# Attention and two expert layers in one kernel: one branch behind the first expert's blocks, another order of the ending, later zeros and weights, and tokens routed in groups of 8, 8, 4, 2 and 2 tiles

## The chip, the cores and the metric

The kernel runs on one core of one Trainium2 chip. The metric is the time of an execution on the device, in microseconds; of several runs the median counts.

## The reference: what is computed

Three layers follow one another. N is 3072 tokens of width 384, there are 8 experts of hidden width 1024, and a dense layer of hidden width 2048.

```python
# 1: gated linear attention, 4 batches x 8 heads, 768 steps, 48 wide
for t in range(S):
    state = alpha[:, :, t, :, None] * state + k[t] (x) v[t]
    y[:, :, t] = q[t] @ state
# 2: each token goes to one expert, the arg max of a cosine
logits = xn @ en.T / tau
expert_idx = argmax(logits); gate_w = softmax(logits)[expert_idx]
out[mask] = gate_w[mask, None] * (relu(x[mask] @ w1[e]) @ w2[e])
# 3: dense layer with an ELU
h = x @ w_in
g = np.where(h > 0.0, h, np.exp(np.minimum(h, 0.0)) - 1.0)
return g @ w_out
```

## The kernel before, in words

**Attention** (`fast`, lines 608 to 707) works on 24 tiles of 128 tokens (6 chunks of time by 4 batches). One pass of its loop serves several tiles at different stages: `load` and `load_v` fetch tile i+3; `stR` and `stA` make running products of alpha for tile i+2 (two scans on VectorE, lines 311 and 321) and multiply k and q with them on GpSimd (`Kh` line 314, `Qh` line 323); `stS` forms scores of tile i+1 (TensorE, line 351) and `stP` masks them (VectorE, line 358); `stC` forms the output of tile i and the update of the state; `stD` turns the output of tile i-1 into rows of the token table and logits (line 419). The loop has 22 passes (i = 0 to 21); `ending` (lines 736 to 793) finishes the last two tiles in an order of its own.

**Routing.** Tiles are routed in groups (`GROUPS`, line 35): five of four and two of two. `stR1` finds each token's expert and its norm, `stR2` its place among the rows of that expert (small matmuls, line 500, and three VectorE instructions), `stX` and `gates` the gate. A group's instructions go into a list `todo`, and each pass takes up to 12 of them. In the loop `stR1` of a group starts two passes after its last tile, `stR2` three passes after it and ahead of `stS` and `stT`, `stX` four passes after it. `scale_x` multiplies a tile's rows with the gate (ScalarE, line 518) and `put` scatters them by an indirect DMA of GpSimd into the table `xs` (line 528), at most one tile a pass.

**Other loads.** At pass 1 SP asks for the first six pieces of expert weights (`load_w`, line 156), at passes 2 to 5 it writes zeros into two experts' parts of `xs` a pass (`fill`, line 543). At passes 4 to 15 a piece of weights is split into a high and a low part (`split_piece`, ScalarE line 172, VectorE line 175), after which the next piece is asked for. Each engine works its own queue in the order of the program; SP's queue issues nearly all loads.

**Into the experts.** Rows of tiles 0 to 21 are read back from `xs` for expert 0 (`load_rows`, line 246); those of the last two tiles come in by a one-hot matmul (`first_x`, line 540), added up in the same PSUM tiles `t0`. Then come two branches that all engines take: line 798 leads to `general` and the filling of rare short experts, line 1111 to `overflow` for an expert with more than 432 tokens. Each begins with a register load on each engine (lines 797 and 1110) from a flag that `pack` computes (lines 820 to 846). Behind them `moe1` (lines 848 to 959) transposes the rows of expert 0 (`turn`, lines 877, 880, 881), and runs 64 blocks (expert e, hidden slice f): `mm1` is the first layer (lines 892 to 898), `mm2` the second (lines 907 to 909), one block later. At f = 6 SP loads a register and copies the expert's token numbers to `idl` (lines 939 and 940). Dense weights come as 64-bit words (`load_d`, line 196) and are decoded on the way. `moe2` is the dense layer; its output goes out by indirect DMAs.

Of the kernel before, what the change touches and what calls it, by code (L numbers as in the profile page):

```python
# [8 lines left out]
F32 = mybir.dt.float32  # L9
# [9 lines left out]
N, DM = B * S, H * D  # L19
# [15 lines left out]
GROUPS = [list(range(i, i + 4)) for i in range(0, 20, 4)] + [[20, 21], [22, 23]]  # L35
# [24 lines left out]
def fused_kernel(ctx, tc, qk, a, v, emb, w12, wi, wo, cst, sel, cols, out):  # L60
# [34 lines left out]
    bad_i = const.tile([1, 1], I32, name="bad_i")  # L95

# [161 lines left out]
    def attention():  # L258
        with ExitStack() as st:
# [14 lines left out]
            rhsX = gp.tile([128, NP, CW + E], F32, name="rhsX")  # L274
            ss = gp.tile([128, NT], F32, name="ss")
            chk = gp.tile([C2, NT, NP, 2], F32, name="chk")
            ones = gp.tile([128, 1], F32, name="ones")
            tick = gp.tile([1, 1], F32, name="tick")
# [162 lines left out]
            todo, putq, urgent, late = [], [], [], []  # L441

# [48 lines left out]
            def stR2(g):  # L491
# [3 lines left out]
                r = ps1.tile([128, 4, E], F32, tag="psT" if g == NG - 2 else "psR", name="psR")[:, :n]  # L495
# [50 lines left out]
            def general():  # L546
# [13 lines left out]
                rv = wk.tile([128, TB, DE], F32, tag="yT", name="row_v")  # L560
# [47 lines left out]
            def fast():  # L608
# [42 lines left out]
                gated = set()  # L651
                last = {tiles[-1]: g for g, tiles in enumerate(GROUPS)}
                tail = NT - 2
                for i in range(tail):
                    load(i + 3)
                    load_v(i + 3)
                    if i == 1:
                        load_w(2 * PIECES)
                    if 2 <= i < 2 + E // 2:
                        for e in (2 * i - 4, 2 * i - 3):  # L660
                            fill(e, zero, FULL if e else 0)
                    if i - 3 in last:
                        todo[:0] = stR2(last[i - 3])
                    stS(i + 1)
                    stT(i + 1)
# [6 lines left out]
                    stP(i + 1, 1)  # L672
                    while late:
                        late.pop(0)()
# [61 lines left out]
            def ending():  # L736
# [4 lines left out]
                r = stR2(g2 - 1)  # L741
                run(urgent, r)
# [54 lines left out]
            odd = nc.values_load(odd_i[0:1, 0:1], min_val=0, max_val=4 * E + C2)  # L797
            with tc.If(odd > 0):
                bad = nc.values_load(bad_i[0:1, 0:1], min_val=0, max_val=C2)
                with tc.If(bad > 0):  # L800
                    with tc.manual_schedule():
                        general()
                        run(pack(sm, ps1))
                zero = wk.tile([128, CAPR], F32, tag="P", name="zero")
                nc.vector.memset(zero, 0.0)
                for e in range(E):
                    n_low = nc.values_load(low_i[0:1, e:e + 1], min_val=0, max_val=FULL // 64)
                    with tc.If(n_low > 0):
                        n_e = nc.values_load(cnt_i[0:1, e:e + 1], min_val=0, max_val=N)
                        with tc.For_i(0, n_low, 1) as s:  # L810
                            row = nc.s_assert_within(n_e + s * 64 + e * REG, 0, E * REG - 64)
# [380 lines left out]
```

## Time and profile before

| | us |
|---|---|
| median of 3 runs | 866.92 |
| lowest and highest | 863.48, 867.87 |
| the profiled execution | 860.85 |
| its span, first to last instruction | 858.9 |

The profile is of one execution. It gives for each engine the time in which it was busy, in all and by stretches, and what ended each wait. PE is TensorE, with PEld its weight loads; DVE is VectorE, ACT ScalarE, POOL GpSimd and SP SyncE; a q behind a name is that engine's queue of register loads, branches and DMA issues. PEclk is the granted clock of TensorE as a share of 2.4 GHz. The stages can be told by their lines: attention up to about 164 us, the ending and the routing of the last tiles up to about 185, the experts from 194 to about 450, and the dense layer after that.

### The profile page before, as it was taken

What the parts mean: (1) busy time and instruction counts of PE and PEld (TensorE: products, weight loads), DVE (VectorE), ACT (ScalarE), POOL (GpSimd) and SP (SyncE); (2) the same over time, 40 slices, a digit from 0 to 9 for tenths busy, and PEclk for the clock granted to TensorE, in tenths of its full rate; (3) what the DMA queues carried; (4) which work ended last, traced back from release to release, by engine and by line L of the source; (5) the groups of instructions that cost most, each with busy time, mean ns of one, the idle gap of its engine ahead of it and who ended that gap; (6) DMA issues with size and microseconds to landing.
All of it is one profiled execution on the core that took longest, in us unless ns stands there. A gap on an engine that the chain in (4) does not pass through costs nothing.

```text
span 858.9 us, 13084 instructions
## 1 busy us (share of the span) xinstructions
PE 803.1 (94%) x4880; PEld 726.0 (85%) x4880; DVE 548.8 (64%) x1054; ACT 361.3 (42%) x763; POOL 200.1 (23%) x218
## 2 busy tenths in 40 slices
PE   7697888859998998999999999999999999999996
PEld 5697877728988988999998889999999999999995
DVE  7699999833676776777636766545545555455442
ACT  2365756522544544545535544333323333333231
POOL 6334656631233333333200002002002001000102
PEclk7798989798999999999999999999999999999999
DMA  9978678231676776778400000000000000000000
GB/s 243 309 223 237 204 214 243 75 111 48 149 195 169 153 202 168 138 240 191 88 1 1 0 1 37 1 1 38 0 1 28 10 1 15 23 0 2 36 1 37
DMA packets 45249, 82.33 MB, mean 96 GB/s; under 512 B 11624, under 2 KB 18024, under 8 KB 45168
## 3 DMA queue, kind: packets, MB, share of 16 engines
q1 hardware_dynamic: 42096, 71.88, 32.1%
q0 software_dynamic: 3072, 9.45, 2.9%
q8 instruction: 41, 0.67, 0.4%
q14 instruction: 40, 0.33, 0.1%
HBM read 69.10 MB, written 12.22 MB: 95 GB/s over the span
## 4 chain that ended last, share of the span: by engine, by line
PE 63%; DMA 5%; DVE 4%; ACT 3%; issue 1%; SPq 0%; POOLq 0%; POOL 0%; DVEq 0%; ACTq 0%
PE h L1044 20%; PE o L1067 7%; PE o L1065 7%; PE o L1066 7%; PE y L907 4%; PE y L908 3%; DMA raw<-in_wi_dram 3%; PE h L892 3%; PE h L894 3%; PE y L909 3%; PE h L893 3%; DMA raw<-in_wo_dram 1%; PE t L875 1%; DVE dlo L231 1%; DVE g L1050 1%
## 5 line engine op out<-in xcount | busy, mean ns | idle before, releaser
L1046 DVE TENSOR_SCALAR mn<-h 128x512 f32<-128x512 f32 x96 | 66.3, 690 | 139.6 <-PE h L1044 139.6
L1047 ACT ACTIVATE mn<-mn 128x512 f32<-128x512 f32 x96 | 60.7, 633 | 171.3 <-DVE mn L1046 171.3
L1067 PE MATMUL o<-dwo,gl 128*128 128x384 f32 x384 | 129.5, 337 | 1.5 <-DVE gl L1054 1.4
L1066 PE MATMUL o<-dlo,gh 128*128 128x384 f32 x384 | 128.3, 334 | 0.0
L1065 PE MATMUL o<-dwo,gh 128*128 128x384 f32 x384 | 128.3, 334 | 0.0
L1076 POOL DMA_INDIRECT out_dram<-ob,ids x24 | 23.5, 981 | 390.7 <-DVE ob L1071 231.6
L1044 PE MATMUL h<-xh,dwi 128*128 128x512 f32 x288 | 112.9, 392 | 0.6 <-ACT x2T L921 0.6
L1044 PE MATMUL h<-xh,dlo 128*128 128x512 f32 x288 | 113.1, 393 | 0.0
L1044 PE MATMUL h<-xl,dwi 128*128 128x512 f32 x288 | 112.5, 392 | 0.0
L1053 ACT ACTIVATE gh<-g 128x512 fp32r<-128x512 f32 x96 | 60.7, 633 | 78.5 <-DVE g L1050 78.5
L897 ACT ACTIVATE hh<-h 128x432 fp32r<-128x432 f32 x64 | 33.9, 530 | 104.7 <-PE h L894 102.6
L1050 DVE SCALAR_TENSOR_TENSOR g<-mn,h 128x512 f32<-128x512 f32 x96 | 66.1, 689 | 15.4 <-ACT mn L1047 15.3
L1065 PEld LDWEIGHTS o<-dwo,gh 128*128 128x128 f32 x384 | 72.0, 187 | 4.2
L1066 PEld LDWEIGHTS o<-dlo,gh 128*128 128x128 f32 x384 | 72.0, 187 | 4.0
L898 DVE SCALAR_TENSOR_TENSOR hl<-h,hh 128x432 fp32r<-128x432 f32 x64 | 38.7, 605 | 55.8 <-ACT hh L897 55.8
L907 PE MATMUL y<-hh,whi 128*128 128x432 f32 x192 | 71.3, 371 | 3.3 <-ACT hh L897 3.3
L175 DVE TENSOR_TENSOR wlo<-raw,whi 128x512 fp32r<-128x512 f32 x96 | 71.4, 768 | 4.5 <-ACT whi L172 4.5
L215 POOL TENSOR_SCALAR dg<-dg 128x384 f32<-128x384 f32 x32 | 40.9, 1279 | 142.9 <-ACT dg L214 142.6
L1067 PEld LDWEIGHTS o<-dwo,gl 128*128 128x128 f32 x384 | 72.2, 188 | 2.4 <-DVE gl L1054 2.1
L908 PE MATMUL y<-hl,whi 128*128 128x432 f32 x192 | 69.2, 360 | 2.9 <-DVE hl L898 2.9
L892 PE MATMUL h<-xh,whi 128*128 128x432 f32 x192 | 69.1, 360 | 0.0
L894 PE MATMUL h<-xh,wlo 128*128 128x432 f32 x192 | 69.1, 360 | 0.0
(204 smaller groups left out, 1581.5 us busy)
## 6 DMA issues: line engine op xcount, KB each, us to landing
raw<-in_w_dram SPq DMA_DIRECT2D x96, 256.0 KB, 3.6
qk<-in_qk_dram SPq DMA_DIRECT2D x24, 448.0 KB, 6.8
vt<-in_v_dram SPq DMA_DIRECT2D x24, 352.0 KB, 6.8
raw<-in_wi_dram SPq DMA_DIRECT2D x16, 384.0 KB, 4.4
raw<-in_wo_dram SPq DMA_DIRECT2D x16, 384.0 KB, 4.4
at<-in_alpha_dram SPq DMA_DIRECT2D x24, 226.2 KB, 4.7
xr<-xs SPq DMA_DIRECT2D x7, 576.0 KB, 11.8
xs<-zero SPq DMA_DIRECT2D x7, 288.8 KB, 7.5
```

The costliest lines, as they stand in the source:

```text
L175: nc.vector.tensor_tensor(l[:, sl], r, h[:, sl].bitcast(F32), op=ALU.subtract)
L892: nc.tensor.matmul(ps, wh, xh[:, kk], start=(kk == 0), stop=False)
L894: nc.tensor.matmul(ps, wl, xh[:, kk], start=False, stop=(kk == KD - 1))
L907: nc.tensor.matmul(acc[e][d], wh, hh, start=(f == 0), stop=False)
L908: nc.tensor.matmul(acc[e][d], wh, hl, start=False, stop=False)
L1044: nc.tensor.matmul(ps, l, x, start=(n == 0), stop=(n == len(terms) - 1))
L1046: nc.vector.tensor_scalar(mn, ps, 0.0, None, op0=ALU.min)
L1047: nc.scalar.activation(out=mn, in_=mn, func=AF.Exp)
L1050: nc.vector.scalar_tensor_tensor(g, mn, -1.0, ps, op0=ALU.add, op1=ALU.max)
L1065: nc.tensor.matmul(o_, gh[:, sl], wh, start=(f == 0), stop=False)
L1066: nc.tensor.matmul(o_, gh[:, sl], wl, start=False, stop=False)
L1067: nc.tensor.matmul(o_, gl[:, sl], wh, start=False, stop=(f == M - 1))
```

## The change

The groups become 8, 8, 4, 2 and 2 tiles. `fill` moves from passes 2 to 5 to passes 4 to 7; the first weight pieces are asked for one a pass from pass 5 to pass 10, and the splits move from passes 4 to 15 to passes 9 to 20. In a pass `stS` and `stT` now come ahead of `stR2`; a pass may scale two tiles and scatter two of them while the list is long. `ending` takes the last tiles in another order. The two branches become one, which comes behind `turn` of expert 0 and the first two blocks of `mm1`; what was behind both now stands in a function `fix`, which, where it runs, makes these blocks anew (`redo`). The flag `odd_i` counts overflowing tokens too. Two pools of `moe1` lie on the other side of the memory, and the pool of dense weights is opened behind the branch. The token numbers are copied by ScalarE's queue.

```diff
-GROUPS = [list(range(i, i + 4)) for i in range(0, 20, 4)] + [[20, 21], [22, 23]]
+GROUPS = [list(range(8)), list(range(8, 16)), list(range(16, 20)), [20, 21], [22, 23]]
...
                 for i in range(tail):
                     load(i + 3)
                     load_v(i + 3)
-                    if i == 1:
-                        load_w(2 * PIECES)
-                    if 2 <= i < 2 + E // 2:
-                        for e in (2 * i - 4, 2 * i - 3):
+                    if 4 <= i < 4 + E // 2:
+                        for e in (2 * i - 8, 2 * i - 7):
                             fill(e, zero, FULL if e else 0)
+                    if 5 <= i < 5 + 2 * PIECES:
+                        load_w()
+                    stS(i + 1)
+                    stT(i + 1)
                     if i - 3 in last:
                         todo[:0] = stR2(last[i - 3])
-                    stS(i + 1)
-                    stT(i + 1)
...
                     stP(i + 1, 1)
+                    if len(putq) > 4 and place[putq[0]][0] in gated:
+                        put(putq.pop(0))
...
-                    if putq and i < tail - 3 and place[putq[0]][0] in gated:
-                        scale_x(putq[0])
-                    for g in [g for j, g in last.items() if i == min(j + 4, tail - 1) and j < tail - 2]:
+                    for j in putq[:2 if len(putq) > 5 else 1]:
+                        if place[j][0] in gated and j not in scaled:
+                            scale_x(j)
+                    for g in [g for j, g in last.items() if i == j + 4]:
...
-                    if 4 <= i < 4 + AHEAD * PIECES:
+                    if 9 <= i < 9 + AHEAD * PIECES:
                         split_piece(lag)
+                putq.extend(GROUPS[NG - 3])
...
-                r = stR2(g2 - 1)
-                run(urgent, r)
+                while putq and place[putq[0]][0] in gated:
+                    put(putq.pop(0))
+                stD(i - 1)
                 stS(i + 1)
                 stP(i + 1, 0)
                 stP(i + 1, 1)
-                run(late)
+                r = stR2(g2 - 1)
+                run(todo, r)
+                todo.clear()
+                stC(i)
+                x3 = stX(g2 - 1)
+                run(x3 + gates(g2 - 1), late)
                 late.clear()
-                while len(putq) > 3:
-                    put(putq.pop(0))
-                stD(i - 1)
-                stC(i)
-                late.pop(0)()
-                run(*stR1(g2))
-                while len(putq) > 1:
+                gated.add(g2 - 1)
+                m2, n2 = stR1(g2)
+                run(m2, n2)
+                for _ in range(2):
                     put(putq.pop(0))
                 stC(i + 1)
                 r = stR2(g2)
...
+            def redo():
+                with tc.tile_pool(name="psF", bufs=2, space=PS) as pool:
+                    for kk in range(KD):
+                        t = pool.tile([128, CAPR], F32, name="t")
...
+                        evict(0, kk, t[:, :CAP])
+                    for f in range(EARLY):
+                        first_layer(pool.tile([128, CAP], F32, name="h"), 0, f)
...
+            EARLY = 2
+            with tc.manual_schedule():
+                for kk in range(KD):
+                    turn(0, kk)
+                for f in range(EARLY):
+                    mm1(0, f)
+            odd = nc.values_load(odd_i[0:1, 0:1], min_val=0, max_val=4 * E + C2 + N)
+            with tc.If(odd > 0):
+                fix(x2T, redo)
+            dense = es.enter_context(tc.tile_pool(name="dense", bufs=18))
...
-                        o3 = nc.sync.value_load(off_i[0:1, e:e + 1], min_val=0, max_val=N)
-                        nc.sync.dma_start(out=idl[bass.ds(o3, CAP)], in_=xs[e * REG:e * REG + CAP, DM:])
+                            o3 = nc.scalar.value_load(off_i[0:1, e:e + 1], min_val=0, max_val=N)
+                            nc.scalar.dma_start(out=idl[bass.ds(o3, CAP)], in_=xs[e * REG:e * REG + CAP, DM:])
```

## Rows read from the trace of the kernel before

**Rows 1.** The page: busy time by engine; granted clock in 40 slices.

```profile
PE 803.1 (94%) x4880; PEld 726.0 (85%) x4880; DVE 548.8 (64%) x1054; ACT 361.3 (42%) x763; POOL 200.1 (23%) x218
...
PEclk7798989798999999999999999999999999999999
```

**Rows 2.** Windows: length, busy us of PE, PEld, DVE, ACT, POOL, clock, DMA.

```profile
25.30:67.20 41.90, 35.11 (x414) 32.18 (x416) 33.16 (x73) 23.36 (x68) 14.17 (x12) 0.88 0.88 260
101.80:130.00 28.20, 24.07 (x274) 22.21 (x273) 27.51 (x62) 17.14 (x51) 16.74 (x16) 0.88 0.75 216
130.00:155.90 25.90, 22.99 (x256) 21.09 (x256) 25.18 (x58) 14.69 (x46) 16.74 (x16) 0.87 0.76 210
61.60:160.00 98.40, 84.67 (x973) 77.72 (x972) 96.09 (x206) 61.63 (x181) 56.92 (x54) 0.90 0.74 210
```

**Rows 3.** VectorE's waits (us, times, longest) and DMA total, early passes.

```profile
DVE R L311 <- DMA at<-in_alpha_dram: 5.4, 2, 3.7
...
DMA packets 6699, 14.36 MB, mean 266 GB/s; under 512 B 722, under 2 KB 2514, under 8 KB 6692
```

**Rows 4.** Groups by line, 60 to 160 us: busy, mean ns, idle before.

```profile
L528 POOL DMA_INDIRECT xs<-xt,pos_i x13 | 22.5, 1729 | 2.1 <-issue 1.3 <-ACT xt L432 0.3 <-ACT sq L435 0.3
...
L175 DVE TENSOR_TENSOR wlo<-raw,whi 128x512 fp32r<-128x512 f32 x11 | 7.5, 680 | 0.0
...
L472 DVE TENSOR_TENSOR lg<-lg,rs_y 128x32 f32<-128x32 f32 x4 | 4.5, 1113 | 0.1
L487 DVE TENSOR_SCALAR gt<-gt 128x4 f32<-128x4 f32 x4 | 4.3, 1087 | 0.1
L507 DVE TENSOR_SCALAR pos_i<-pos 128x4 int32<-128x4 f32 x3 | 3.1, 1042 | 0.1
...
L488 DVE RECIPROCAL gt<-gt 128x4 f32<-128x4 f32 x4 | 0.7, 178 | 0.1
```

**Rows 5.** Timeline at 99.9 us: start, length, engine, line, instruction.

```profile
99.89 1.26 DVE L487 TENSOR_SCALAR gt<-gt 128x4 f32<-128x4 f32 x1
...
99.93 1.19 POOL L323 TENSOR_TENSOR Qh<-qk,A 112x512 f32<-112x512 f32 x1
```

**Rows 6.** TensorE's timeline at 183 us, then the chain of waits.

```profile
183.29 1.72 PE L540 MATMUL t<-hot,xt 128*128 128x432 f32 x4
...
193.73 6.30 PE t L877 x24
...
203.80 0.20 PE y L907
...
214.43 0.53 PE t L875 x4
```

**Rows 7.** TensorE's queue by line: ns minimum/median/maximum, first and last start.

```profile
L797 PEldq TENSOR_LOAD <-odd_i x1: 490/490/490, 183.8 to 183.8; - x1
...
L798 PEldq COMPARE_BRANCH  x1: 3362/3362/3362, 184.4 to 184.4; - x1
...
L1111 PEldq COMPARE_BRANCH  x1: 4773/4773/4773, 188.5 to 188.5; - x1
```

**Rows 8.** Windows behind the branches, columns as in rows 2.

```profile
190.00:194.00 4.00, 0.27 (x1) 0.30 (x2) 0.00 (x0) 0.00 (x0) 0.00 (x0) 0.50 0.06 9
200.00:202.00 2.00, 2.00 (x11) 1.88 (x11) 0.61 (x1) 0.53 (x1) 0.00 (x0) 1.00 0.42 79
```

**Rows 9.** GpSimd's timeline at the end of attention.

```profile
160.47 1.19 POOL L323 TENSOR_TENSOR Qh<-qk,A 112x512 f32<-112x512 f32 x1
...
175.92 0.96 POOL L528 DMA_INDIRECT xs<-xt,pos_i  x1 [0.21 <-issue]
...
177.18 0.96 POOL L528 DMA_INDIRECT xs<-xt,pos_i  x1 [0.22 <-issue]
...
185.57 0.96 POOL L528 DMA_INDIRECT xs<-xt,pos_i  x1 [7.34 <-DMA xr<-xs]
```

**Rows 10.** SP's queue, line 940, columns as in rows 7.

```profile
L940 SPq DMA_DIRECT2D idl<-xs x8: 576/590/637, 223.3 to 422.0; - x8
```

More of the change, by code (lines that the diff above doesn't have):

```diff
@@ L95, in fused_kernel @@
     bad_i = const.tile([1, 1], I32, name="bad_i")
+    rhsX = const.tile([128, NP, CW + E], F32, name="rhsX")
+    ss = const.tile([128, NT], F32, name="ss")
+    tick = const.tile([1, 1], F32, name="tick")
     def inv_norm(pool, x):
@@ L441, in attention @@
             todo, putq, urgent, late = [], [], [], []
+            gated = set()
             def step(n=1):
@@ L494, in stR2 @@
                 s3 = [128, n, E]
-                r = ps1.tile([128, 4, E], F32, tag="psT" if g == NG - 2 else "psR", name="psR")[:, :n]
+                r = ps1.tile([128, 8, E], F32, tag="psT" if g == NG - 2 else "psR", name="psR")[:, :n]
                 o_ = oh[:, i0:i0 + n]
@@ L887, in mm1, with first_layer @@
             def mm1(e, f):
-                ps = psG.tile([128, CAP], F32, tag="g", name="h")
+                hb[e, f] = (h_p.tile([128, CAP], F32R, tag="hh", name="hh"),
+                            h_p.tile([128, CAP], F32R, tag="hl", name="hl"))
+                first_layer(psG.tile([128, CAP], F32, tag="g", name="h"), e, f)
+            def first_layer(ps, e, f):
                 xh, xl = xT[e]
@@ L959, in moe1 @@
-            return first
+            EARLY = 2
+            with tc.manual_schedule():
+                for kk in range(KD):
[6 more added lines that the diff above has]
+            dense = es.enter_context(tc.tile_pool(name="dense", bufs=18))
+            psA = st.enter_context(tc.tile_pool(name="psA", bufs=1, space=PS))
@@ new lines, in moe1 @@
+            psT = st.enter_context(tc.tile_pool(name="psT", bufs=2, space=PS))
+            dc = st.enter_context(tc.tile_pool(name="dc", bufs=2))
+            with tc.manual_schedule():
+                load_d(0, dc)
+                load_d(1, dc)
+                load_x(1)
+                LAG = 1
+                blocks = [(e, f) for e in range(E) for f in range(FB)]
+                for n in range(EARLY - 1, len(blocks) + LAG):
+                    if n < len(blocks):
+                        e, f = blocks[n]
+                        if n >= EARLY:
+                            mm1(e, f)
+                        if f == 6:
+                            o3 = nc.scalar.value_load(off_i[0:1, e:e + 1], min_val=0, max_val=N)
+                            nc.scalar.dma_start(out=idl[bass.ds(o3, CAP)], in_=xs[e * REG:e * REG + CAP, DM:])
+                        if f >= 4 and f < 4 + KD:
+                            turn(e + 1, f - 4)
+                    if n >= LAG:
+                        mm2(*blocks[n - LAG])
+                    if n > 2:
+                        split_piece()
+                        if n % 2:
+                            split_piece()
+                    if freed:
+                        load_d(freed.pop(), dc)
+                    j = (n - 2) * 4 // 7
+                    if j >= 0 and j != (n - 3) * 4 // 7:
+                        decode(j, dc, dense)
+                        freed.append(j + 2)
+                    if n > len(blocks) - 4:
+                        split_dense("wi", n - len(blocks) + 3, dense)
+                        if n > len(blocks) - 2:
+                            split_dense("wo", n - len(blocks) + 1, dense)
@@ L961, in split_x @@
+            return first, dense
     def split_x(x2T, xh, xl, u, kk):
@@ L1109, in fused_kernel @@
         x2T = p.tile([128, KD, N + CAP], F32, name="x2T")
-        over = nc.values_load(over_i[0:1, 0:1], min_val=0, max_val=N)
-        with tc.If(over > 0):
-            with tc.manual_schedule():
-                overflow(x2T)
+        first, dense = moe1(x2T, *x0, es)
+        shared.close()
         with tc.manual_schedule():
-            dense = es.enter_context(tc.tile_pool(name="dense", bufs=18))
-            first = moe1(x2T, *x0, dense)
-            shared.close()
             moe2(x2T, first, dense)
```

108 lines of the change are left out of this document (42 added, 66 removed).

## The prediction

> **What bounds the kernel now.** I read the page first: TensorE is busy for 803.1 us of the 858.9 us span, and its granted clock dips only in the first quarter [rows 1]. So a gain can only come from that quarter: attention, routing, and the step into the first expert. I then cut it at the starts of the 24 `R` scans, which open the passes of the attention loop. The windows by pass [rows 2] are to be read by which engine fills them. Passes 2 to 7 take 41.9 us, of which VectorE is busy for 33.16; passes 13 to 16 and 17 to 20 take 28.2 and 25.9 us, and VectorE is busy for 27.51 and 25.18 of them. So the early passes wait for something, and the later ones are VectorE's. TensorE is near behind: 84.67 us of work in 98.4 us, which is 14.5 passes, at a mean clock of 0.90; that is 84.67 x 0.90 / 14.5 = 5.25 us a pass at 2.4 GHz.
>
> What the early passes wait for is in VectorE's waits and in the DMA total [rows 3]: the scan waits 5.4 us for alpha, while 14.36 MB move at 266 GB/s. What fills VectorE later is in the groups by line [rows 4]. Beside its scans it runs 29 small routing instructions for every four tiles (lines 104 to 116 and 462 to 507). Three of them, L487, L472 and L507, have means of 1.04 to 1.11 us, where L488, on the same 128x4 elements as L487, has 0.18. With 0.17 for the other 26 (an estimate from that row) a routing is 3 x 1.08 + 26 x 0.17 = 7.7 us. The timeline shows what stretches the three [rows 5]: L487 starts at 99.89 and lasts as long as GpSimd's `Qh` product beside it.
>
> At the other end, the chain has TensorE idle from 185.0 (end of L540, 183.29 + 1.72) to 193.73, where the 24 transposing matmuls of the first expert begin [rows 6]. The queue rows name the cause [rows 7]: the two branches, 3.4 and 4.8 us on TensorE, each behind a register load. The granted clock has fallen to 0.50, that is 1.2 GHz, by 190 and is back at 2.4 GHz by 200 [rows 8].
>
> **The change, part by part.**
>
> *Later weights and zeros.* Up to pass 7 the six first pieces (0.26 MB each) and the four that their splits fetch are 2.62 MB. After, only the three of passes 5 to 7 are asked for by then: 1.83 MB less, at 266 GB/s 6.9 us [rows 3]. The zeros are the same bytes two passes later. Passes 2 to 7 also lose their 26 routing instructions and four splits of 0.68 us [rows 4]. Their floor by TensorE is 6 x 5.25 + 1.1 for the second `psX` of pass 2 = 32.6 us, or 9.3 us under 41.9. I take **-7.0** (bounds -2 and -9.3), by the bytes, since passes 4 to 7 now carry zeros and weights. On SP's queue both stand behind alpha, q, k and v of their pass and ahead of those of the next; they are hidden while the loads run a pass ahead of their use.
>
> *Groups of eight.* Two routings of the loop go. Passes 9 to 12 route the first eight tiles in the place of four: the same 29 instructions, some nine of them 32 elements longer, **+0.3**. Passes 13 to 16 route nothing, and what is late next sets them: TensorE at 5.25 us, or GpSimd where two scatters fall into one pass, two products of 1.19 [rows 5] and two scatters of 1.73 [rows 4], with the gaps some 6.0 us. Two such passes and two others are 22.5 us against 28.2: **-5.7** (bounds 0 and -8.4: VectorE's own work, 27.51 less one routing of 7.7). Passes 17 to 20 route tiles 8 to 15 and keep four splits that were earlier in passes 4 to 7: 4 x 0.68 + 0.3 = **+3.0**. Pass 21 loses five of 17 routing instructions, one of them long: **-1.0**. The position matmuls, now behind `stS` and `stT` on TensorE, save 0, as VectorE fills the passes that have them. Loop: -7.0 + 0.3 - 5.7 + 3.0 - 1.0 = **-10.4**.
>
> By the Trainium skill ("SBUF — State Buffer", its bullet on the shared port pair) a GpSimd instruction and certain VectorE ones exclude each other for a whole instruction. [rows 5] agree. It speaks against the change: the GpSimd work stays, so by the rule the long waits may pass to the next VectorE instruction, and the sum below would be -11.6 in the place of -15.3, the first rival.
>
> *The ending.* Scores and masks of tile 23 now come ahead of the routing of tiles 16 to 19, so the chain to the last gates can be some 3 us earlier. But the expert's rows are read only after the scatters of tiles 0 to 21. Before, the last `Qh` ends at 161.7; nine scatters are left, they wait for gates, and the last ends at 178.14 [rows 9]. After, gates open later, so one scatter of pass 21, six of tiles 10 to 15, four and two are left, and only GpSimd's pace counts: 13 x 1.26 (177.18 - 175.92) from 161.7 is 178.1. So **0** (bounds -2.9, the earlier chain, and +4, if five of them last 1.73 as in the loop).
>
> *One branch behind the first blocks.* Before, 203.80 - 185.01 = 18.8 us lie between the end of L540 and the first `y` matmul [rows 6]. After, the rows have landed at 185.6, since GpSimd's next scatter, which waits for that read, starts at 185.57 [rows 9]. The 24 transposing matmuls go at full clock, 24 x 0.133 (L875, 0.53 for four) = 3.2, in the place of 6.30 at half; the two first-layer blocks take 3.8 (203.80 - 200.03). So TensorE reaches the branch at 192.6. Then a register load of 0.5, one branch of 3.4 and 0.4 to the first matmul [rows 7]: 196.9. ScalarE, VectorE and SP take the same branch at about that time; GpSimd is behind its two last scatters and has decoding as its next work. Queued behind it on SP are two loads of dense words and the rows of expert 1. A halt of 4.3 us may again bring the half clock: before, it cost half of the 6 us from 193.73 to about 200 [rows 8], or 3.0; I take 2.0, as the halt is half as long. 198.9 in the place of 203.8 is **-4.9** (bounds -0.6, with the branch of 4.8 and 5.9 us lost to the clock and to code that comes late, and -8.0 with no dip, the branch starting 0.6 sooner and the rows not waited for).
>
> *Ids by ScalarE.* Eight register loads (0.5 us [rows 7]) and DMA issues (0.59 us each on SP [rows 10]) now stand among the evictions, one to an expert; behind them wait an eviction and, through it, VectorE and TensorE. They are hidden by the block that TensorE works ahead, 3.8 us with both layers [rows 6]: **0** (bounds 0 and +8.7, all of it exposed). The first loads of dense words stand behind the branch on SP: 0, as their first use comes two blocks later (bound +4.3, one more halt).
>
> Sum: -10.4 + 0 - 4.9 = **-15.3**. The profiled execution, 860.85 us, gives 845.5; the median of the runs shown is 6.07 above it, so I predict 866.92 - 15.3 = **851.6 us**.
>
> **The rivals.** *The wait is handed on*: the scans and masks take over the waits for GpSimd that the routing had. The three long instructions of a routing are each 0.9 us over a short one, 2.7 together; passes 13 to 16 then gain 3.0 and pass 21 nothing, loop -6.7, total -11.6: 855.3 us. For it: GpSimd's products are as many as before. Against: all waits cannot move, since VectorE would have gaps in which GpSimd runs alone.
>
> *The branch stays exposed*: late loads on SP make its code as slow to come as the second branch before, and the clock falls again: -0.6 there, 855.9 us.
>
> *The early passes gain nothing*, since the zeros only move the jam to passes 4 to 7, so that this part does not do what it is for: total -8.3, 858.6 us.
>
> *All covers hold*: -9.3 in passes 2 to 7, -2.9 in the ending, -8.0 at the branch, total -23.6: 843.3 us.
>
> *Slower, by the clock*: passes without routing leave TensorE waiting for `Qh` and it drops to 1.2 GHz, where a pass takes 10.5 us in the place of 5.25. It decides from four such passes on (15.3 + 4.3 = 19.6, by 5.25); with five it is 851.6 + 26.3 = 877.9 us. For it: the clock of 0.87 to 0.88 in [rows 2]. Against: a pass with less for VectorE leaves TensorE fewer gaps.
>
> **How the numbers follow.** My forecast has 0.45, within 847 to 856; the wait handed on 0.16, the exposed branch 0.12, no early gain 0.07, all covers 0.16, slower 0.04. From 842 to 861 holds 8 in 10: it takes in all covers on one side and the single losses on the other. A measurement of this kernel tells about 0.5%, or 4.3 us, from no change: below 862.6 lies 0.90, within it 0.06, above it 0.04.
>
> **What would show it.** Right: pass 2's scan does not wait for alpha; passes 2 to 7 in about 35 us, 13 to 16 in about 22.5; one TensorE branch of 3.4 to 4.8 us behind 18 first-layer matmuls; the transposing matmuls at full clock. Wrong: passes 13 to 16 above 26 us, TensorE at 1.2 GHz in them, the last scatter ahead of the rows later than the loop's end by more than 18 us, or new idle time of TensorE in the experts.

## The result and the profile after

| us | before | after |
|---|---|---|
| median of 5 runs each | 866.61 | 855.97 |
| lowest and highest | 863.48, 867.87 | 854.84, 860.15 |
| the profiled execution, its span | 860.85, 858.9 | 854.84, 852.7 |

The ratio of after to before is 0.9905, with a 95% interval of 0.9877 to 0.9933. Predicted was 851.6 within 842 to 861. The direction was right, but the gain of the medians, 10.6 us, is smaller than the 15.3 of the sum, and the steps of the sum were not all right. In a later set of runs, on another chip, the same code had 0.9871 (0.9851 to 0.9891).

First the windows of the profile after, cut as in [rows 2] at the `R` scans (columns as there): passes 2 to 7, pass 8, 9 to 12, 13 to 16, 17 to 20.

```profile
25.90:64.70 38.80, 35.12 (x420) 32.28 (x418) 28.79 (x43) 21.84 (x63) 14.16 (x12) 0.91 0.78 209
64.70:71.50 6.80, 5.23 (x70) 4.77 (x69) 4.64 (x7) 3.45 (x10) 2.36 (x2) 1.00 1.05 286
71.50:96.90 25.40, 21.11 (x258) 19.53 (x258) 24.71 (x60) 13.97 (x40) 9.45 (x8) 0.93 0.80 217
96.90:123.10 26.20, 22.40 (x272) 20.52 (x268) 24.82 (x34) 19.13 (x56) 19.14 (x19) 0.93 0.86 252
123.10:150.20 27.10, 21.50 (x288) 19.41 (x286) 26.40 (x62) 17.85 (x53) 13.21 (x12) 1.00 0.71 209
```

Passes 2 to 7 fell from 41.9 to 38.8 us, 3 and not 7, and pass 8, to which the prediction gave nothing, grew from 5.8 to 6.8. Passes 13 to 16, which route nothing now, still take 26.2 (28.2 before), and VectorE is still busy for 24.82 of them with 34 instructions where it had 62. Passes 9 to 12, where I expected +0.3, fell from 28.95 to 25.4.

Next, DMA in passes 2 to 8 of after, busy tenths in 40 slices, then two waits in the same stretch, of SP's queue and of VectorE (us, times, longest), then SP's timeline (start, length).

```profile
DMA  9992004797200089888978999999999999999999
...
DMA packets 4817, 10.06 MB, mean 221 GB/s; under 512 B 471, under 2 KB 2263, under 8 KB 4811
...
SPq L299 <- PE psU L382: 13.5, 2, 7.2
...
DVE R L311 <- DMA at<-in_alpha_dram: 5.4, 3, 2.2
...
25.01 0.31 SPq L293 DMA_DIRECT2D qk<-in_qk_dram  x1
32.56 0.35 SPq L299 DMA_DIRECT2D vt<-in_v_dram  x1
33.00 0.94 SPq L291 DMA_DIRECT2D at<-in_alpha_dram  x1
34.02 0.38 SPq L293 DMA_DIRECT2D qk<-in_qk_dram  x1
40.86 0.35 SPq L299 DMA_DIRECT2D vt<-in_v_dram  x1
41.25 1.42 SPq L544 DMA_DIRECT2D xs<-zero  x2
```

DMA is nearly idle twice, for 7 of 40 slices of 1.14 us in all, and nearly full from then on. SP stands twice for about 7 us with the load of v at its head, until TensorE has read the buffer; alpha, k and q of the next tile stand behind it, and the zeros too. VectorE's scan still waits 5.4 us for alpha, as before [rows 3], but now where passes 6, 7 and 8 open, no longer where passes 3 and 4 do.

In passes 13 to 16, the groups of VectorE (busy us, mean ns) and a piece of the two timelines:

```profile
L178 DVE TENSOR_TENSOR wlo<-raw,whi 128x512 fp32r<-128x512 f32 x5 | 7.7, 1543 | 0.0
L311 DVE TENSOR_TENSOR_SCAN R<-at,back 112x517 f32<-112x517 f32 x5 | 6.8, 1370 | 1.2 <-DMA at<-in_alpha_dram 1.2
...
101.44 2.13 DVE L178 TENSOR_TENSOR wlo<-raw,whi 128x512 fp32r<-128x512 f32 x1
...
101.83 1.19 POOL L323 TENSOR_TENSOR Qh<-qk,A 112x512 f32<-112x512 f32 x1
```

The split, 680 ns in [rows 4], has a mean of 1543: it starts beside GpSimd's scatter and ends half a microsecond after the `Qh` product does (101.83 + 1.19 = 103.02; 103.57). The routing instructions that waited so in [rows 5] are gone from these passes, and the split waits in their place.

At the end of attention TensorE halts in the output of tile 22, for no wait that the profile shows (engine, line, what ended it: us, times, longest); the rows of expert 0 are read 29.2 us after the scan of pass 21 (179.39 - 150.2), where before had 24.0.

```profile
PEld psY L374 <- issue: 5.2, 7, 1.3
...
179.39 2.14 SPq L249 DMA_DIRECT2D xr<-xs  x4
```

Into the experts, TensorE's timeline, the queue rows of the one branch (columns as in [rows 7]) and the clock behind it (as [rows 8]):

```profile
181.42 1.72 PE L541 MATMUL t<-hot,xt 128*128 128x432 f32 x4
182.98 3.61 PE L893 MATMUL t<-cs,xr 128*128 128x128 f32 x24
...
196.33 0.70 PE L939 MATMUL y<-hh,whi 128*128 128x432 f32 x1 [6.00 <-DVEq L965]
...
L965 PEldq COMPARE_BRANCH  x1: 3926/3926/3926, 188.8 to 188.8; - x1
...
L965 DVEq COMPARE_BRANCH  x1: 72/72/72, 191.6 to 191.6; - x1
...
196.00:200.00 4.00, 3.67 (x10) 3.43 (x11) 0.00 (x0) 0.00 (x0) 0.00 (x0) 0.50 0.19 49
```

From the end of the one-hot matmuls to the first `y` it is now 196.33 - 183.14 = 13.2 us (18.8 before). The transposing matmuls take 3.61 us where they took 6.30, at a granted clock of 1.00. The halt that is left is 6.0 us, and a granted clock of 0.50, that is 1.2 GHz, follows it.

### The profile page after: what moved, and what is told of

Same layout as the page of the kernel before. It is cut to its first block, busy times and chain, and to the rows that moved or that the text cites. A ratio compares the mean times of both kernels' runs of the same rounds, so it can differ in the third digit from the quotient of the medians.

```text
span 852.7 us, 12999 instructions
## 1 busy us (share of the span) xinstructions
PE 797.6 (94%) x4876; PEld 718.6 (84%) x4876; DVE 541.7 (64%) x997; ACT 360.5 (42%) x761; POOL 193.8 (23%) x218
## 4 chain that ended last, share of the span: by engine, by line
PE 65%; DVE 4%; DMA 4%; ACT 2%; issue 1%; POOLq 0%; POOL 0%; SPq 0%; DVEq 0%; ACTq 0%
PE h L1088 20%; PE o L1111 7%; PE o L1109 7%; PE o L1110 7%; PE y L939 4%; PE y L940 4%; PE y L941 4%; PE h L911 3%; PE h L909 3%; PE h L910 3%; DMA raw<-in_wi_dram 2%; PE t L891 1%; DVE dlo L234 1%; DMA raw<-in_wo_dram 1%; DVE g L1094 1%
## 5 line engine op out<-in xcount | busy, mean ns | idle before, releaser
L1120 POOL DMA_INDIRECT out_dram<-ob,ids x24 | 23.5, 981 | 368.7 <-DVE ob L1115 171.1
L178 DVE TENSOR_TENSOR wlo<-raw,whi 128x512 fp32r<-128x512 f32 x96 | 77.5, 831 | 5.9 <-ACT whi L175 5.0
L941 PE MATMUL y<-hh,wlo 128*128 128x432 f32 x192 | 69.4, 361 | 0.0
```

Source lines behind the costliest of these rows:

```text
L178: nc.vector.tensor_tensor(l[:, sl], r, h[:, sl].bitcast(F32), op=ALU.subtract)
L941: nc.tensor.matmul(acc[e][d], wl, hh, start=False, stop=(f == FB - 1))
```

## The experiments

Runs of one set share a chip and the runs of the kernel before. The medians of before differ from chip to chip (856.6, 855.9 and 858.4 us here, 866.6 in the section on the result), so ratios to before are compared. Each has an interval of about ±0.0025, so a difference between two has some ±3 us.

### Set 1: one part undone at a time

**Early timing** (`old_timing`):

```diff
-                    if 4 <= i < 4 + E // 2:
-                        for e in (2 * i - 8, 2 * i - 7):
+                    if i == 1:
+                        load_w(2 * PIECES)
+                    if 2 <= i < 2 + E // 2:
+                        for e in (2 * i - 4, 2 * i - 3):
...
-                    if 5 <= i < 5 + 2 * PIECES:
-                        load_w()
...
-                    if 9 <= i < 9 + AHEAD * PIECES:
+                    if 4 <= i < 4 + AHEAD * PIECES:
```

> The kernel after with the zeros (passes 2 to 5), the first six weight pieces (asked for at pass 1) and the splits (passes 4 to 15) where the kernel before has them; all else as after. By my theory now, the early passes are held by the bytes of all loads together: in the profile after, the scan of pass 9 starts at 71.5 (before: 73.0), though four routing passes were gone as well, so later loads gave little there, and the four late splits cost VectorE up to 3.0 us in passes 17 to 20. So I expect the scan of pass 9 at 70.5 to 73, passes 17 to 20 2 to 3 us shorter than the 27.1 of after, and a time between 3 us below and 1 us above the kernel after (ratio to before 0.987 to 0.992). The rival is the term of my sum (-7.0 by the bytes taken out of passes 2 to 7): the scan of pass 9 then starts at about 78 and the time is 3 to 4 us above the kernel after (ratio 0.994 to 0.996).

Measured: ratio 0.9798 (0.9773 to 0.9824), median 838.6 us. Pass 9 starts at 67.4 and passes 17 to 20 take 25.4. Windows of passes 2 to 8 and 9 to 20, and DMA's slices in the first of them:

```profile
25.60:67.40 41.80, 39.33 (x474) 36.08 (x475) 36.23 (x54) 27.10 (x76) 16.55 (x14) 0.92 0.92 272
67.40:143.80 76.40, 66.29 (x804) 60.85 (x802) 74.86 (x151) 48.35 (x141) 41.71 (x39) 0.93 0.76 220
...
DMA  9899999999999979999998994899867988948998
```

Neither expectation holds: pass 9 starts earlier than both had it. Passes 2 to 8 move more (272 GB/s and 11.38 MB) in less time, since DMA hardly idles. Later loads gained neither 7 us nor nothing: against 0.9871 they cost about 6.

**Groups of four** (`groups_of_four`):

```diff
-GROUPS = [list(range(8)), list(range(8, 16)), list(range(16, 20)), [20, 21], [22, 23]]
+GROUPS = [list(range(i, i + 4)) for i in range(0, 20, 4)] + [[20, 21], [22, 23]]
```

> The kernel after with the groups of the kernel before (five of four tiles, two of two); later loads, ending and branch as after. Passes 5 to 8 then route again, and 13 to 16 too. By the theory that the wait for GpSimd is handed on, the split on VectorE (mean 1543 ns in passes 13 to 16 after, 682 before) takes over part of it, so two routings less are worth some 4 to 7 us, not 15.4 (two of 7.7): ratio 0.995 to 0.999, and the splits in passes 13 to 16 have a mean under 1.0 us again. By the term of my sum, passes 13 to 16 lose 5.7 and more: 7 to 10 us, ratio 0.999 to 1.002. By the rival that all of it is handed on, the time stays as after: 0.989 to 0.992.

Measured: 0.9934 (0.9909 to 0.9959), 5.4 us slower than 0.9871. Windows of passes 9 to 12 and 13 to 16, and the split in the latter:

```profile
72.00:100.40 28.40, 21.60 (x262) 19.92 (x262) 27.71 (x61) 16.58 (x50) 16.77 (x15) 0.94 0.85 220
100.40:128.50 28.10, 23.45 (x290) 21.49 (x290) 27.41 (x62) 19.96 (x58) 16.72 (x16) 0.94 0.73 215
...
L178 DVE TENSOR_TENSOR wlo<-raw,whi 128x512 fp32r<-128x512 f32 x5 | 3.4, 683 | 0.0
```

With routing back in passes 13 to 16, the split is at 683 ns again. So the wait is handed on, as the first theory had it, though the ratio lies just below the range that was given for it.

**Branch ahead of the blocks** (`branch_first`):

```diff
             EARLY = 2
+            odd = nc.values_load(odd_i[0:1, 0:1], min_val=0, max_val=4 * E + C2 + N)
+            with tc.If(odd > 0):
+                fix(x2T, lambda: None)
             with tc.manual_schedule():
...
-            odd = nc.values_load(odd_i[0:1, 0:1], min_val=0, max_val=4 * E + C2 + N)
-            with tc.If(odd > 0):
-                fix(x2T, redo)
```

> The kernel after with its one branch put ahead of the transposing matmuls and the first two blocks, and nothing made anew behind it (that path isn't taken); all else as after. In the profile after, 13.2 us lie between the end of the last one-hot matmul (183.14) and the first second-layer matmul (196.33), of which 6.0 are the halt at the branch, and the clock is 0.50 to 0.90 in the 8 us behind it, which costs 1.3. If the place of the branch matters as I predicted, its halt adds to the reading of the rows only in part, the transposing matmuls run at half clock (6.3 for 3.6) and the first y comes 15 to 17 us after the one-hot matmuls: 1 to 3 us slower than after, ratio 0.992 to 0.994. If joining the two branches is all that counts and their place nothing: ratio 0.989 to 0.991. If code coming late behind it makes the halt as long as the second branch before: first y 17 to 19 us behind, 4 to 5 us slower, ratio 0.995 to 0.997.

Measured: 0.9854 (0.983 to 0.9878), no slower than after. TensorE's timeline and its branch:

```profile
182.62 6.54 PE L893 MATMUL t<-cs,xr 128*128 128x128 f32 x24 [4.11 <-PEq L960]
194.22 0.36 PE L939 MATMUL y<-hh,whi 128*128 128x432 f32 x1
...
L960 PEldq COMPARE_BRANCH  x1: 4292/4292/4292, 177.9 to 177.9; - x1
```

The first `y` comes 15.7 us after the one-hot matmuls (194.22 - 178.51), as expected. But the nine `y` matmuls follow at 0.20 us apart, where after has 0.36 behind its halt, so about 1.6 of the 2.5 us come back (195.99 - 194.22 against 199.71 - 196.33). The place of the branch is worth nothing that this measurement can tell.

**Order of the ending as before** (`old_ending`; the two hunks of `ending` and the loop's end undone):

```diff
-                while putq and place[putq[0]][0] in gated:
-                    put(putq.pop(0))
-                stD(i - 1)
+                r = stR2(g2 - 1)
+                run(urgent, r)
...
-                x3 = stX(g2 - 1)
-                run(x3 + gates(g2 - 1), late)
```

> The kernel after with the order of the ending of the kernel before (and the gates of tiles 16 to 19 made at the end of the loop, as there); all else as after. From the scan of pass 21 to the issue of the rows of expert 0 the profile before has 24.0 us (156.06 to 180.06), the profile after 29.2 (150.2 to 179.39): the loop ended 5.9 us earlier and the rows are read only 0.7 earlier. If the new order is the cause, the old one gives back 3 to 5 us: the stretch is 24 to 26 us, ratio 0.985 to 0.987. If the scatters left over for the ending set it (six of the second group, four and two, with groups of eight), the stretch stays at 28 to 30: ratio 0.989 to 0.992. If it is the halting of TensorE at the output of tile 22 (161.1 to 166.2, by code that comes late, as no wait is shown), the halt goes or moves with the order and the stretch shortens by what it cost, at most 4 us.

Measured: 0.9862 (0.984 to 0.9884), and 25.3 us from pass 21 to the rows (150.9 to 176.24), without the halts. It looked like the third case, until the next run.

### Set 2: what the later loads ran into

**The kernel after, unchanged** (`after_again`):

> The kernel after, unchanged, beside the three others of this set and with a profile of its own. In the first profile of it TensorE halts seven times in the output of tile 22 (4.5 us of weight loads that wait for nothing shown, 161.1 to 166.2), and the rows are read 29.2 us after the scan of pass 21; the four kernels of the first set, whose code differs elsewhere, have no such halt there and 24.2, 25.1, 24.9 and 25.3 us. If the halt belongs to where this kernel's code lies, it is there again, 3 to 5 us long, the stretch is 28 to 30 us, and the ratio is 0.988 to 0.993, as first measured. If it was chance in one execution, it is gone, the stretch is about 25 us, and the ratio of this set is 0.985 to 0.988.

Measured: 0.9871, with 24.0 us from the scan of pass 21 (149.6) to the rows and none of the halts:

```profile
25.80:70.70 44.90, 40.18 (x485) 36.82 (x486) 33.80 (x51) 25.29 (x73) 16.54 (x14) 0.92 0.80 218
70.70:149.60 78.90, 66.70 (x806) 61.09 (x808) 77.40 (x153) 51.07 (x146) 41.68 (x39) 0.94 0.79 226
...
173.63 2.14 SPq L249 DMA_DIRECT2D xr<-xs  x4
```

So the halts do not belong to this code as such, and the order of the ending is worth nothing measurable (0.9862 against 0.9871).

**Zeros early, weights late** (`zeros_early`):

```diff
-                    if 4 <= i < 4 + E // 2:
-                        for e in (2 * i - 8, 2 * i - 7):
+                    if 2 <= i < 2 + E // 2:
+                        for e in (2 * i - 4, 2 * i - 3):
```

> The kernel after with the zeros at passes 2 to 5 again; weights and splits stay as late as after. With zeros, weights and splits all as before, passes 2 to 8 took 41.8 us (25.6 to 67.4), after 45.6 (25.9 to 71.5), with DMA almost idle in 5 of 40 slices of the latter, in passes 2 to 4. If that idle time is the cause, the zeros (8 transfers, the larger part of what was moved) fill it, and passes 2 to 8 take 41 to 43 us; the time is 2 to 4 us below the kernel after. If the weights are the cause, passes 2 to 8 stay at 44.5 to 46 and the time is within 1.5 us of after. Passes 17 to 20 stay at 26 to 27.5, as they keep their splits.

Measured: 0.9787 (0.9764 to 0.981), 7 us below after_again, more than expected. Passes 2 to 8 take 43.2 us (25.4 to 68.6), and the scan of pass 21 starts at 146.2 in the place of 149.6. By the times the zeros were the part that mattered; the profiles place only 3.4 of the 7 us in the loop, and where the rest lies is not shown.

**Five buffers for v** (`vt_five`):

```diff
-            VB = 4
+            VB = 5
```

> The kernel after with five buffers for v in the place of four. In the profile after, SP's queue waits 13.5 us in passes 2 to 8 with the load of v at its head, for the matmuls that read the tile four before, and alpha, k and q of the next tile stand behind it while DMA idles. If this wait is why the idle time is not used, a fifth buffer lets the loads run ahead: SP's waits for v fall to under 4 us, DMA idles in two slices or fewer of passes 2 to 8, and pass 9 starts 2 to 4 us earlier than the 71.5 of after. If the three buffers of alpha, k and q hold the loads in any case, the wait only moves to them and pass 9 starts within 1 us of 71.5.

Measured: 0.9786 (0.9765 to 0.9808), median 837.86. Windows of passes 2 to 7 and of pass 8, the wait of SP's queue in passes 2 to 8, and SP's timeline:

```profile
25.60:59.70 34.10, 31.94 (x371) 29.46 (x371) 28.95 (x43) 19.77 (x57) 13.40 (x12) 0.90 0.91 257
59.70:64.90 5.20, 5.20 (x70) 4.81 (x70) 4.93 (x9) 3.44 (x12) 2.36 (x3) 1.00 1.05 259
...
SPq L299 <- PE psU L382: 3.0, 2, 1.7
...
32.68 3.74 SPq L544 DMA_DIRECT2D xs<-zero  x2
```

One more buffer undoes the loss, and more than expected: the zeros of pass 4 are issued at 32.68 in the place of 41.25, the wait for v falls from 13.0 us (after_again) to 3.0, the scan no longer waits for alpha in passes 2 to 8, and pass 9 starts at 64.9 in the place of 70.7. Passes 5 to 8 then take 5.2 us each, with TensorE busy throughout at full clock. That is the 5.25 that the prediction had as TensorE's floor.

**Splits away from the scatters** (`splits_early`, on top of the early timing):

```diff
-                    if 4 <= i < 4 + AHEAD * PIECES:
-                        split_piece(lag)
+                    if 3 <= i < 1 + AHEAD * PIECES:
+                        for _ in range(2 if i in (8, 11) else 1):
+                            split_piece(lag)
```

> The kernel with the early timing (the kernel after with the zeros and weights of before, 0.9798 of the time before), with its twelve splits in passes 3 to 12 (two in passes 8 and 11), so that none stands beside GpSimd's scatters. There the split took 1753 ns on average in passes 13 to 16 (five of them), against 682 without a wait, and the four passes 25.4 us. If only instructions like the split wait for GpSimd, passes 13 to 16 fall to TensorE's and GpSimd's own pace, 21 to 22.5 us, with the scans at 1.2 to 1.3 us as they were; the time is 2 to 4 us below the kernel with early timing (ratio 0.975 to 0.978). If the wait is handed on once more, to the scans, these grow to some 1.9 us in the mean and the four passes take 23.5 to 25.4; the time is within 1.5 us of the kernel with early timing (0.978 to 0.982). Passes 8 and 11 may be up to 1 us longer each in both cases.

Measured: 0.9813 (0.979 to 0.9835), 1.3 us above early timing. Passes 13 to 16 take 23.5 us (25.4 there). Two of VectorE's groups from 93 to 120 us, and one scan beside `Qh`:

```profile
L311 DVE TENSOR_TENSOR_SCAN R<-at,back 112x517 f32<-112x517 f32 x5 | 8.4, 1681 | 1.8 <-ACT yT L376 1.0 <-DMA at<-in_alpha_dram 0.7
...
L358 DVE TENSOR_TENSOR P<-psS,cs 128x512 f32<-128x512 f32 x9 | 6.1, 675 | 0.0
...
115.95 2.76 DVE L311 TENSOR_TENSOR_SCAN R<-at,back 112x517 f32<-112x517 f32 x1 [1.05 <-ACT yT L376]
...
116.43 1.19 POOL L323 TENSOR_TENSOR Qh<-qk,A 112x512 f32<-112x512 f32 x1
```

The wait is handed on once more: a `R` scan of 1.23 us takes 2.76 and ends 1.1 us behind `Qh`. What is won in passes 13 to 16 is lost elsewhere: passes 2 to 8, which got more of the splits, take 45.6 us (41.8 there), though why they take so much longer is not shown.

### Set 3: the branch alone, the chips, and both cures

**The joined branch alone** (`branch_only`; in the kernel after, the loop, the groups, the ending and SP's copy of the token numbers are those of before; the diff is against before):

```diff
-            odd = nc.values_load(odd_i[0:1, 0:1], min_val=0, max_val=4 * E + C2)
-            with tc.If(odd > 0):
...
+            with tc.manual_schedule():
+                for kk in range(KD):
+                    turn(0, kk)
+                for f in range(EARLY):
+                    mm1(0, f)
+            odd = nc.values_load(odd_i[0:1, 0:1], min_val=0, max_val=4 * E + C2 + N)
+            with tc.If(odd > 0):
+                fix(x2T, redo)
```

> The kernel before with the joined branch alone, behind the transposing matmuls and the first two blocks; groups of four, timing, ending, loop and the copy of the token numbers as before. My term for the branch was -4.9 us (bounds -0.6 and -8.0): ratio 0.9943. From the profiles, the first second-layer matmul comes 16.3 us after the issue of expert 0's rows in the kernel after (second profile) and 23.6 in the kernel before, with up to 2 us given back to the half clock behind the halt: 5 to 6 us, ratio 0.993 to 0.994. By the rival that the branch stays exposed, -0.6 us: 0.998 to 1.000. The kernel with early timing (0.9798) is this one with groups of eight and the new ending; what lies between the two is what the groups are worth with early loads: by my theory 10 to 13 us, where they are worth 5.4 with the late ones (0.9934 to 0.9871).

Measured: 0.9934 (0.9912 to 0.9957), that is -5.7 us of 858.42. The first `y`, then the windows of passes 2 to 8 and 9 to 20, which stand against those of early timing above:

```profile
199.52 0.70 PE L932 MATMUL y<-hh,whi 128*128 128x432 f32 x1 [4.49 <-DVEq L958]
...
26.10:72.10 46.00, 41.70 (x466) 38.29 (x468) 39.43 (x84) 25.94 (x74) 16.58 (x14) 0.86 0.84 239
72.10:155.50 83.40, 71.29 (x826) 65.19 (x822) 80.81 (x181) 52.43 (x154) 50.40 (x47) 0.90 0.71 211
```

With early loads the groups shorten the loop by 4.2 and 7.0 us, 11.2 together; the ratios give 11.7 (0.9934 to 0.9798). One more comparison lies in these runs: groups of four with the late loads (set 1) also had 0.9934. So with groups of four the later loads cost nothing measurable, and the 6 us that they cost appear only with groups of eight. Groups of four still route in passes 5 to 8; that this is what hides the late loads is not shown.

**The kernel before, for a profile on this chip** (`before_profile`, no edit):

> The kernel before, unchanged, for a profile on this chip: its runs here are 856 us where they were 867, so the passes must be compared on one chip. If the chips differ in the transfers, passes 2 to 8 are shorter than the 47.6 us of the first profile (by up to 5 us, since halts of 4.8 us for late code stood there too) and the passes from 9 on the same within 1 us (83.1 us from pass 9 to pass 21). If they differ all over, every stage is shorter by 1.2%.

Measured, one run of 862.38 us. Passes 2 to 8 take 46.9 us (25.5 to 72.4; 47.6 first), 9 to 20 82.3 (83.1 first). So the early passes are shorter by 0.7, not 5. The rows are read 26.7 us after the scan of pass 21 (24.0 first), and from the first `y` to the end it is 651.1 us (860.0 - 208.95) in the place of 655.1. What is shorter here lies mostly behind attention, which neither expectation has. But this execution is not shorter as a whole than the first profile (862.38 against 860.85 us), so it does not show where the 8 us lie by which the medians of before differ.

**Five buffers, early zeros, weights spread** (`five_and_spread`):

```diff
-            VB = 4
+            VB = 5
...
-                    if 4 <= i < 4 + E // 2:
-                        for e in (2 * i - 8, 2 * i - 7):
+                    if 2 <= i < 2 + E // 2:
+                        for e in (2 * i - 4, 2 * i - 3):
...
-                    if 5 <= i < 5 + 2 * PIECES:
+                    if 4 <= i < 4 + 2 * PIECES:
...
-                    if 9 <= i < 9 + AHEAD * PIECES:
+                    if 7 <= i < 7 + AHEAD * PIECES:
```

> The kernel after with five buffers for v, zeros at passes 2 to 5, weights asked for one a pass from pass 4 and splits in passes 7 to 18. Five buffers alone gave 0.9786, the early zeros alone 0.9787, against 0.9871 for the kernel after. If both only undo the same idle time of DMA, they don't add up: ratio 0.976 to 0.980, with passes 5 to 8 at TensorE's 5.2 us as with the five buffers, and 1 to 2 us from two splits less in passes 17 to 20. If each had a cause of its own: 0.969 to 0.973.

Measured: 0.9846 (0.982 to 0.9871), slower than either cure alone and outside both expectations.

**Five buffers, early timing** (`five_and_early`; the edits of `old_timing` and `vt_five`):

> The kernel after with five buffers for v and with zeros, weights and splits as early as in the kernel before. With four buffers this timing gave 0.9798, five buffers with the late timing 0.9786. If the early timing already fills what the fifth buffer would open, the ratio stays at 0.977 to 0.981. If SP's wait for v (8.2 us in passes 2 to 8 there) still cost something, passes 2 to 8 fall from 41.8 to 38 to 40 us: ratio 0.974 to 0.977. If the loads, now ahead, collide with all the weights, alpha comes late and it is slower: over 0.982.

Measured: 0.9819 (0.9794 to 0.9843), between the first expectation and the last. In both kernels the loop is hardly worse: the scan of pass 21 starts at 144.0 and 143.7, against 143.3 with five buffers alone. So in the loop the two cures don't add up; both kernels moved weights and splits as well, and five buffers with early zeros alone were not run. What is worse is the ending, 29.1 and 28.9 us from there to the rows. The kernel with weights spread has the halts of the first profile after:

```profile
PEld psY L374 <- issue: 4.1, 7, 1.2
...
173.15 2.15 SPq L249 DMA_DIRECT2D xr<-xs  x4
```

All four kernels of this set have a long ending (26.7 to 29.1 us; 24.0 to 25.3 in sets 1 and 2), the kernel before among them. So these two ratios cannot simply be set against those of set 2. The best times are those of five buffers alone, of the early zeros and of the early timing, 2.0 to 2.1% under before, which can't be told from each other.

## Why the prediction was right, and which of its steps were wrong

| step | predicted us | measured us |
|---|---|---|
| one branch behind the first blocks | -4.9 | -5.7 (branch alone) |
| groups of eight, in the loop: +0.3 - 5.7 - 1.0 | -6.4 | -5.4 with late loads, -11.7 with early |
| later zeros, weights and splits: -7.0 + 3.0 | -4.0 | +6.2 with groups of eight (0.9798 to 0.9871), 0 with groups of four (0.9934 twice) |
| order of the ending | 0 | 0 within ±3 |
| by profile: passes 2 to 7 | -7.0 | -3.0 and -3.9 |
| pass 8 | 0 | +1.0 and +1.2 |
| passes 9 to 12 | +0.3 | -3.5 and -3.0 |
| passes 13 to 16 | -5.7 | -2.0 and -2.3 |
| passes 17 to 20 | +3.0 | +1.2 and +1.2 |

The first rows undo parts of the change; they don't cut it as the sum does, whose -7.0 was for passes 2 to 7 as a whole, with the routing that leaves them. The rows by profile cut it so: first profile before against the first and the second of after. By them passes 2 to 20 gained 6.3 and 6.8 us of the 9.4 forecast. Pass 21's -1.0 was not measured by itself.

Branch, groups with early loads and later loads make -11.2, beside the -11.0 that 0.9871 is of 855.9; this is no check, as the three steps are one chain of ratios with these ends. Errors of opposite sign cancelled in part: the forecast had too large a gain in passes 2 to 8 and 13 to 16, too small a one in passes 9 to 12, and too large a loss in passes 17 to 20. So that the time fell inside the range is in part luck. It lies nearest to two rivals, at 855.3 and 855.9 us: the first one's wait in passes 13 to 16 did happen, the second one's exposed branch did not. One of the prediction's own signs of being wrong, passes 13 to 16 above 26 us, came true in the first profile of after (26.2; 25.8 in the second).

**One branch.** Right in size and mostly in mechanism. From the one-hot matmuls to the first `y` the working had 11.9 us (196.9 - 185.01); it was 13.2 in after and 11.7 with the branch alone (199.52 - 187.84), and the dip to 1.2 GHz came too. That the first `y` of after stands at 196.33, near the 196.9 of the working, is luck: the one-hot matmuls ended 1.9 us earlier, and the halt was 6.0 us in the place of 4.3. Two things were not in it. TensorE's queue ran ahead and took its branch at 188.8, while its matmuls still ran; the halt was ended by VectorE, which reached the branch only at 191.6, behind its evictions, and went on at 196.2. Its branch has 72 ns on record, but 4.6 us pass until it goes on (4.4 with the branch ahead of the blocks, 177.9 to 182.3), so an engine that comes late to the branch holds up TensorE. And the place behind the blocks is worth nothing measurable; so the 5.7 us are put down to the joining.

By the Trainium skill ("Runtime: NRT & Kernel Launch", Instruction fetch mechanics) a branch whose target lies outside the code already fetched has to fetch it first. TensorE's branches of 3.4 to 4.8 us fit that; no row here shows the fetch itself.

**Later zeros and weights.** This is the step that failed, as "I take **-7.0** (bounds -2 and -9.3), by the bytes": passes 2 to 7 gained 3.0 and 3.9 us by the two profiles, and pass 8 lost 1. The bytes did fall, from 12.10 MB (passes 2 to 8 before) to 10.06, but 266 GB/s is a rate of a DMA that hardly idles, and in these passes it fell from 254 to 221. What went wrong is "they are hidden while the loads run a pass ahead of their use": SP's queue did not run ahead, since it waited with the load of v for a buffer. The same rows before (DMA and the wait of SP's queue in passes 2 to 8, then SP's timeline):

```profile
DMA  9999999999999974899998953988715878708998
...
SPq L299 <- PE psU L382: 5.3, 2, 4.1
...
19.41 5.29 SPq L156 DMA_DIRECT2D raw<-in_w_dram  x6
...
28.13 1.42 SPq L543 DMA_DIRECT2D xs<-zero  x2
...
34.30 1.34 SPq L543 DMA_DIRECT2D xs<-zero  x2
```

Before, the weights and the first zeros were issued ahead of the long wait and filled DMA in passes 2 and 3. After, the zeros and three weight pieces fall into passes 4 to 7, and the scans of passes 6 to 9 wait for alpha. The rival "the early passes gain nothing, since the zeros only move the jam" had this mechanism, and with its chance of 0.07 was held too unlikely; in size passes 2 to 8 gained 2.0 and 2.7 us, not 0, but the routing that left them is in that gain. Against the early timing the late loads lost 3 to 4 us there (41.8 against 44.9 and 45.6). That early zeros and a fifth buffer each remove the loss is shown.

**Passes 13 to 16.** The term of -5.7 measured -2.3 (28.10 with groups of four, 25.80 in the second profile after). The rival "the wait is handed on", which gave -3.0 here, happened. Groups of four with the split at 683 ns, groups of eight with 1543, and the `R` scan at 2.76 us once no split stands there, show it. The argument against it, that VectorE would have gaps, was wrong, as VectorE stays the fullest engine of these passes.

By the Trainium skill ("SBUF — State Buffer", SBUF: two separate sides) a GpSimd instruction that reads that memory excludes a VectorE one with both inputs in it. The trace agrees: split and scan, which have two such inputs, end 0.55 and 1.1 us behind `Qh` where they meet it, while the masks, which read PSUM, stay at 0.67 us.

**Passes 9 to 12.** Predicted +0.3, measured -2.4 (28.40 to 26.00, the same pair). The scatters of a group of eight begin only in pass 13, so here routing has no scatters beside it (GpSimd has 8 instructions in these passes, 15 with groups of four). The move of the first scatter was in the change, but not costed:

```profile
L473 DVE TENSOR_TENSOR lg<-lg,rs_y 128x64 f32<-128x64 f32 x1 | 0.6, 585 | 0.0
L488 DVE TENSOR_SCALAR gt<-gt 128x8 f32<-128x8 f32 x1 | 0.5, 511 | 0.0
```

These two, in passes 9 to 12 of after, are two of the long ones in [rows 4], at 1113 and 1087 ns there.

**Passes 17 to 20.** Predicted +3.0 for four more splits and the longer routing; measured +1.2 from before (25.9) to after (27.1), and +1.7 from early timing (25.4), which has one split there where after has five.

**The ending.** 0, and nothing measurable it was: 24.0 us in the second profile, as before. In the first it was 29.2, with the halts; so profile against profile the change shows 6.0 us, and the medians 10.6. In set 3 the old order took 26.7 and 27.4 us and the new one 28.9 and 29.1, so a loss of some 2 us is not excluded.

**Token numbers by ScalarE.** Taken as 0. The eight register loads (273 to 286 ns) and issues (550 ns in the median) are in ScalarE's queue; what they cost was not tried alone.

## What to carry to other kernels

Before moving loads later, look whether DMA idles in the early slices and what the issuing queue waits for at its head; a load that waits for a buffer holds everything behind it, and here one more buffer was worth as much as an earlier order (0.9786 and 0.9787). What a move of loads costs can hang on the other parts of the change: here 6 us with groups of eight and nothing with groups of four. An instruction that is long because it waits for another engine gives back only a part of its length when it is removed: the engine it waited for is still as busy, and the next instruction of the same kind takes the wait.

## What was not expected

TensorE's halts in the output of tile 22: three profiles of this ending have them (5.2 us of weight loads in the first profile after, 4.1 and 2.0 in the last two kernels), seven don't, among them the same code a second time. No wait is shown, nor that code comes late there, as an expectation has it; the granted clock falls to 0.50 behind them (166.2 to 170.2 in the first profile). The ending of the unchanged kernel before differs too: it took 24.0 and 26.7 us in its two profiles, on two chips. What sets it stays open; it can be as large as the term that one wants to measure, so one profile was not enough to judge the ending.
